# Two transfers for the fourth k-tile of each load, a moved sum in the seven-product blocks, and a buffer of its own for the next layer's norm

## The chip, the cores and the metric

The kernel runs on one core of a Trainium2 chip. The metric is the device time of one execution in microseconds, the median of several runs. The core has five engines with their own instruction streams: PE (matrix multiply), DVE (vector), ACT (scalar), POOL (GpSimd) and SP, which here only issues DMA transfers. An engine runs its stream in order, and waits on semaphores that other engines and transfers raise.

## The reference

```
x = x + attention(layernorm(x)); x = x + ffn(layernorm(x))      # this pair twice, same weights
attention: q = x @ wq (16 heads of 28), k = x @ wk, v = x @ wv (one key/value head of 28)
           softmax(q k^T / sqrt(28)) v for each head, then @ wo
ffn:       (silu(x @ w_gate) * (x @ w_up)) @ w_down
x: 2048 x 448, wq: 448 x 448, wk, wv: 448 x 28, w_gate, w_up: 448 x 1792, w_down: 1792 x 448, all float32
```

## The kernel before

**Numbers.** A float32 factor is carried as a rounded high part and a low part (the rest), and a product is high x high + high x low + low x high: `xh`, `xl` for activations, `wh`, `wl` (or `wgh`, `wgl`) for weights. `split` makes both parts on POOL.

**k-tiles.** The contraction length is 448 = 3 x 128 + 64. The fourth k-tile has only 64 rows, and is put into the 128 partitions twice: the upper copy turns into the low part (`flipped`, k = 3), so that one matmul of 128 rows does high and low together. `rows3` loads such a matrix: one transfer for the first three k-tiles, and a second one for the fourth, which reads the same 64 rows twice. It loads the gate and up weights (`columns`), the attention weights (`load_wqkv`) and, from DRAM, the transposed activations (`load` in `norm_steps`).

**Stages.** The tokens are four column groups c of 512. A layer has a projection stage (`Attention.project`, `product_T`: eleven matmuls for one of 16 (c, m) pairs), an attention stage of 256 steps, and a feed-forward stage in `groups` of two 128-column pieces of w_gate and w_up. In the attention stage ACT works nearly without a pause on the exponentials.

**Feed-forward.** The first two groups and the last one run as `unit` (group, c, piece): products into two banks, Silu into the one buffer `sg` on ACT (L1106), times up on DVE (L1107), high part `h` on ACT (L1108), low part on DVE (L1111), then the product with w_down (L345). `between` is a fence: ACT copies one column of a bank into `seen` (L352), and PE's next matmuls on the other rows of that bank wait for it. The four groups between are `mixed`: two column groups a, b at once in a seven-product (Strassen-Winograd) scheme, 16 blocks in a layer. The order within a block is the hand-written list `ORDER`; a name with one "-" at its end belongs to the block before, with two to the one before that, and each name goes to its engine in that order. A1 to A4 and S0 to S5 are products on the banks x, y, z, w (in pairs of 64 rows: the upper and lower half of the array), E and F the products with w_down. The sums out of the banks (C12, C22, C21; L859) run on DVE; C21 reads bank w, into which A2 of the next block writes. silB, mulB, hhB, hlB are the Silu, the product with up, the high part (ACT, L874) and the low part (DVE, L878) of column group b; silA, mulA, hhA, hlA those of a.

**Hand-over.** In the last group of layer 0 `hand_over(c)` prepares the next layer's first norm. For c = 0 it works on the side: statistics, `apply` (DVE, L254) and `turn` (a transpose on DVE, L259) through the buffer `sg`, `send` to DRAM (`xt`, L268), `load` back into `xn` by `rows3` (L128, L129), and `cut`, four casts on ACT into `xh` (L303), one k-tile each, with the low parts on DVE (L308, L311). `self.soon` says after how many units each step is issued. Behind `cut` in ACT's stream stand the `seen` copies of the next unit.

**Start.** Rows of x and the attention weights are loaded by SP in order, then the rows of c = 1 (`fill(1)`, L1250). PE runs idle transposes, transposes the norm of c = 0 (L295), then `project` for c = 0. `part` makes wh on ACT (L209) and wl on DVE (L210); z = 1 is the half that the first two projections use.

Of the kernel before, what the change touches and what calls it, by code (L numbers as in the profile page):

```python
# [8 lines left out]
F32 = mybir.dt.float32  # L9
F32R = mybir.dt.float32r  # L10
AF = mybir.ActivationFunctionType
ALU = mybir.AluOpType
# [3 lines left out]
P = 128  # L16
S = 2048
D = 448
# [34 lines left out]
def forward(  # L53
# [14 lines left out]
    nc = tc.nc  # L68
# [9 lines left out]
    pers = ctx.enter_context(tc.tile_pool(name="pers", bufs=1))  # L78
# [6 lines left out]
    phase, banks, threes, live, turn = ExitStack(), [], [], set(), {}  # L85
# [38 lines left out]
        nc.sync.dma_start(dst.bitcast(F32), src.bitcast(F32))  # L124

    def rows3(dst, src):
        n = src.shape[1]
        nc.sync.dma_start(dst[:, 0:3], src[0:384, :].rearrange("(k p) n -> p k n", p=P))  # L128
        nc.sync.dma_start(dst[:, 3], src[384:448, :][None].to_broadcast([2, 64, n]))  # L129

    def in_turn(cols):

# [18 lines left out]
    qraw = pers.tile([P, 512], F32, name="qraw")  # L151
# [33 lines left out]
    def load_wqkv(pool, first):  # L185


        wh = pool.tile([P, 4, 512], F32R, name="wh")
        wl = pool.tile([P, 4, 512], F32R, name="wl")

        def load(z):
            if first and not z:
                r = halves("wq2").bitcast(F32).rearrange("p a (b n) -> p (a b) n", n=256)
            else:
                r = wpool.tile([P, 4, 2, P], F32, name="wr").rearrange("p k b n -> p k (b n)")
            nc.gpsimd.memset(r[:, :, 252:256], 0.0)
            rows3(r[:, :, 0:224], wq[:, 224 * z : 224 * z + 224])
            rows3(r[:, :, 224:252], wk if z else wv)
            return r

        def part(z, r, k0=0, k1=4, only=None):
            ks = slice(k0, k1)
            hi, lo = (w[:, :, 256 * z : 256 * z + 256].rearrange("p k (b n) -> p k b n", b=2) for w in (wh, wl))
            for i, (cols, n0, n1) in enumerate(((r[:, ks, 0:224], 0, 112), (r[:, ks, 224:256], 112, 128))):
                if only not in (None, i):
                    continue
                raw = cols.rearrange("p k (b n) -> p k b n", b=2)
                if first:
                    nc.scalar.copy(hi[:, :, :, n0:n1], raw)  # L209
                    nc.vector.tensor_tensor(lo[:, :, :, n0:n1], raw, hi[:, :, :, n0:n1], ALU.subtract)  # L210
                else:
                    split(hi[:, ks, :, n0:n1], lo[:, ks, :, n0:n1], raw)

        if first:
            r1, r0 = load(1), load(0)
            return [lambda: part(1, r1), lambda: part(0, r0)], (wh, wl)
        raw = {}
        fs = []
        for z in (1, 0):
            fs.append(lambda z=z: raw.update({z: load(z)}))  # L220
            for kn in ((0, 2, 0), (2, 4, 0), (0, 4, 1)):
                fs.append(lambda z=z, kn=kn: part(z, raw[z], *kn))
        return fs, (wh, wl)
# [6 lines left out]
            again,  # L230
        )

    def norm_steps(c, away=False):


        got = {}
        cs = slice(4 * c, 4 * c + 4)

        def stat(t):
            nc.vector.bn_stats(stats[:, 4 * c + t, :], xres[:, 4 * c + t, :])  # L240
            nc.vector.bn_aggr(mv[:, 4 * c + t, :], stats[:, 4 * c + t, :])

        def scale():
            rstd = pers.tile([P, 4], F32, name="rstd", bufs=2)
            nc.gpsimd.tensor_scalar(rstd, mv[:, cs, 1], 1.0, EPS, ALU.mult, ALU.add)
            nc.gpsimd.tensor_tensor(rstd, rstd, halfn, ALU.pow)
            got["r"] = rstd

        def apply(t):
            if t == 0:  # L250
                got["x"] = pers.tile([P, 4, 512], F32, name="xn")
            got["o"] = (pers.tile([P, 512], F32, name="sg") if away else got["x"][:, t, :])[:, 0:D]
            i, r = xres[:, 4 * c + t, :], got["r"][:, t : t + 1]
            nc.vector.tensor_scalar(got["o"], i, mv[:, 4 * c + t, 0:1], r, ALU.subtract, ALU.mult)  # L254
            if not away:
                nc.gpsimd.tensor_copy(got["x"][:, t, D:512], got["o"][:, 384:D])

        def turn(t):
            nc.vector.transpose(side()[:, :, :, t], got["o"].rearrange("p (k s) -> p k s", s=32))  # L259

        def side():
            return got["x"].rearrange("p t n -> p (t n)")[:, 0 : 4 * D].rearrange("p (k s t) -> p k s t", s=32, t=4)

        def send():
            turns.append(dram.tile([D, 512], F32, name=f"xt{len(turns)}"))
            got["xt"] = turns[-1]
            for a in range(4):
                nc.sync.dma_start(  # L268
                    got["xt"].rearrange("(k r) n -> r k n", r=32)[:, :, P * a : P * a + P],
                    side()[32 * a : 32 * a + 32].rearrange("p k s t -> p k (s t)"),  # L270
                )

        def load():
            got["raw"] = pers.tile([P, 4, 512], F32, name="xn")
            rows3(got["raw"], got["xt"])

        got["load"] = load
        fs = [lambda t=t: stat(t) for t in range(4)] + [scale]
        for t in range(4):
            fs += [lambda t=t: apply(t)] + [lambda t=t: turn(t)] * away  # L280
        return fs + [send] * away, got

    turns = []

# [29 lines left out]

        return [(a[0][rs], b[0][rs]), (a[0][rs], b[1][rs]), (a[1][rs], b[0][rs])]

    def product_T(po, a_h, a_l, tiles):

        xh, xl = tiles[:2]
        seq = []  # L320
        for k in range(3):
            seq += [(a_h[k], xh[:, k, :]), (a_h[k], xl[:, k, :]), (a_l[k], xh[:, k, :])]
        seq += [(a_h[3], xh[:, 3, :]), (a_l[3], xh[:, 3, :])]
        for i, (a, b) in enumerate(seq):
            nc.tensor.matmul(po, a, b, start=(i == 0), stop=(i == len(seq) - 1))  # L325
# [30 lines left out]
    class Attention:  # L356
# [174 lines left out]
        def q(self, c, m):  # L531
            cs = slice(512 * c, 512 * c + 512)
            held, po = bank((3, 4, 5) if self.seen > len(self.order) - 4 else wide[-1], True)
            ms = slice(P * m, P * m + P)
            wh, wl = self.w
            product_T(po, [wh[:, k, ms] for k in range(4)], [wl[:, k, ms] for k in range(4)], self.X[c])
            if not full and self.seen in (6, 10, 14):
                self.maxima(self.seen // 4 - 1)
            live.remove(held)
# [3 lines left out]
            raw = pers.tile([P, 512], F32, name="sg") if last else self.pool.tile([P, 512], F32, name="stage")  # L543
# [45 lines left out]
        def scores(self, ff):  # L589
            next(switch)  # L590
            with tc.tile_pool(name=f"at{self.layer}", bufs=1, reuse_waits="tile") as wp:
# [123 lines left out]
                later = {}  # L715
                for c in range(3):
                    ff.X[c] = xtile(xpool) if c < 2 else None
                    fs, got = norm_steps(c, True)
                    n = NT * (4 * c + 5)
                    for kt, f in enumerate(fs):  # L720
                        later[n + kt] = f
                    later[n + 22] = got["load"]
                    for k in range(4) if c < 2 else ():
                        for z in range(2):
                            later[n + 34 + 2 * k + z] = lambda c=c, got=got, k=k, z=z: flipped(
                                ff.X[c], k, got["raw"][:, k, :], nc.vector.tensor_copy, (z,)
                            )
# [45 lines left out]
    HALVES = slice(0, 64), slice(64, 128)  # L773

    ORDER = (
        "A1 C21- Fc2-- Fp2-- mulA- A2 fY fX Fa0-- Fa1-- A3 fZ fW Fc3-- Fp3-- A4 s1 hhA- u2 E1- w1 w5 fE- u3 S0 "
        "hlA- gY E2- Ea0- Ea1- Ec2- Ep2- Ec3- Ep3- w2 S1 gX S2 gZ S3 gW S4 F1- C12 C22 silB mulB fF- S5 hhB hlB F2- silA"
    ).split()

    class FeedForward:  # L780
# [251 lines left out]
        def hand_over(self, c):  # L1032

            a = self.nxt
            fs, got = norm_steps(c, c == 0)
            for f in fs[:5]:
                f()
            a.pool = self.stage
            a.X[c] = xtile(xpool if c < 2 else self.xbp)

            def ready():
                for f in fs[5:]:
                    f()
                a.norms[c] = got

            if c == 0:
                self.soon.append([1, lambda: [f() for f in fs[5:9]]])
                self.soon.append([2, lambda: [f() for f in (*fs[9:], got["load"])]])
                self.soon.append([4, lambda: cut(got, a.X[c])])
                self.soon.append([5, lambda: [a.project() for _ in range(3)]])  # L1050
            elif c == 1:
                self.soon.append([2, ready])
            else:
                a.plan[4 * c - 4, 0] = [ready]
# [122 lines left out]
        def rest(self, xb):  # L1177
# [21 lines left out]
            for gi, fs in enumerate(groups):  # L1199
# [4 lines left out]
                if gi in mixed:  # L1204
                    self.blocked(gi)
                    if gi == mixed[-1]:
                        nc.gpsimd.memset(qraw, 0.0)
                        mixing.close()
                for c in range(NC) if gi not in mixed else ():
                    for n in range(len(fs)):  # L1210
# [28 lines left out]
    fs, got = norm_steps(0)  # L1239
# [28 lines left out]
    for c in range(1, NC):  # L1268
        fs, got = norm_steps(c)
        n = 4 * c - 4  # L1270
# [38 lines left out]
```

## Time and profile before

| | |
|---|---|
| median of 3 runs | 1973.86 us (1972.9 to 1975.1) |
| the profiled execution | 1975.62 us, of it 1973.8 us span from the first to the last instruction |
| granted TensorE clock, mean | 0.998 |
| PE busy | 1954.8 us, 99% of the span |
| ACT, DVE, POOL busy | 1339.0, 1028.5, 764.7 us |
| transfers | 79.67 MB; SP's queue takes 14.0% of the 16 DMA engines' span |

A row of the timeline gives the start and the duration in microseconds, engine, line, operation, output <- input, shapes, the count of merged instructions, and in brackets the idle time before it with what ended it. PEld is PE's weight load ahead of a matmul. A row of the waits gives total, times and the longest. A row of the stages by window gives the stretch and its length, busy time of PE, PEld, DVE, ACT and POOL (with instruction counts), the granted PE clock, the busy share of the 16 DMA engines and GB/s.

### The profile page before, as it was taken

What the parts mean: (1) busy time and instruction counts of PE and PEld (TensorE: products, weight loads), DVE (VectorE), ACT (ScalarE), POOL (GpSimd) and SP (SyncE); (2) the same over time, 40 slices, a digit from 0 to 9 for tenths busy, and PEclk for the clock granted to TensorE, in tenths of its full rate; (3) what the DMA queues carried; (4) which work ended last, traced back from release to release, by engine and by line L of the source; (5) the groups of instructions that cost most, each with busy time, mean ns of one, the idle gap of its engine ahead of it and who ended that gap; (6) DMA issues with size and microseconds to landing.
All of it is one profiled execution on the core that took longest, in us unless ns stands there. A gap on an engine that the chain in (4) does not pass through costs nothing. (4 is left out here: it accounts for less than half of the span.)

```text
span 1973.8 us, 45469 instructions
## 1 busy us (share of the span) xinstructions
PE 1954.8 (99%) x18315; PEld 1317.0 (67%) x18315; DVE 1028.5 (52%) x1713; ACT 1339.0 (68%) x2353; POOL 764.7 (39%) x988
## 2 busy tenths in 40 slices
PE   9999999999999999999899999999999999999998
PEld 7544545445458999999884445454454688999997
DVE  7444543544435566666554445435454346667653
ACT  4899897997954344444348998979979533444442
POOL 4212111132215768766332222111322157677640
PEclk9999999999999999999999999999999999999999
DMA  5101120121210110011131111101112101110102
GB/s 165 54 20 32 25 50 22 31 59 28 72 33 2 53 32 26 23 32 27 51 97 45 31 31 31 44 12 46 44 37 63 33 5 49 32 32 18 31 17 77
DMA packets 97630, 79.67 MB, mean 40 GB/s; under 512 B 23654, under 2 KB 80614, under 8 KB 97414
## 3 DMA queue, kind: packets, MB, share of 16 engines
q1 hardware_dynamic: 97126, 76.26, 14.0%
q8 instruction: 144, 2.36, 0.5%
q14 instruction: 72, 0.59, 0.1%
q10 hardware_dynamic: 288, 0.46, 0.1%
HBM read 57.15 MB, written 18.74 MB: 38 GB/s over the span
## 5 line engine op out<-in xcount | busy, mean ns | idle before, releaser
L669 PE MATMUL bank<-pt,vsb 128*32 128x512 f32 x4096 | 493.3, 598 | 0.3
L628 PE MATMUL bank<-qstack,keys 32*128 32x512 f32 x1536 | 484.7, 425 | 0.0
L628 PE MATMUL three<-qstack,keys 32*128 32x512 f32 x4608 | 460.3, 425 | 1.5 <-DVE vt L562 1.2
L628 PEld LDWEIGHTS three<-qstack,keys 32*128 32x128 f32 x4608 | 253.9, 182 | 295.4 <-ACT pt L641 179.4
L635 ACT ACTIVATE pt<-three 128x1536 f32<-128x1536 f32 x256 | 372.2, 1454 | 1.1 <-PE bank L669 0.8
L641 ACT ACTIVATE pt<-three 128x1536 f32<-128x1536 f32 x256 | 372.1, 1454 | 0.0
L345 PE MATMUL bank<-xh,wgh 64*128 64x512 f32 x1344 | 359.5, 393 | 6.3 <-ACT seen L352 5.8
L345 PE MATMUL bank<-wdh,h 64*128 64x448 f32 x1776 | 329.7, 364 | 0.4 <-ACT seen L352 0.3
L637 DVE COPY raw<-bank 128x512 f32<-128x512 f32 x256 | 177.5, 693 | 226.7 <-PE bank L628 224.9
L345 PE MATMUL bank<-xh,wgl 64*128 64x512 f32 x1020 | 288.9, 391 | 0.0
L679 DVE TENSOR_TENSOR o<-bank,o 128x512 f32<-128x512 f32 x224 | 155.0, 692 | 240.7 <-PE bank L669 235.8
L669 PEld LDWEIGHTS bank<-pt,vsb 128*32 128x32 f32 x4096 | 107.1, 109 | 249.6 <-issue 152.6
L708 POOL TENSOR_TENSOR o<-o 128x512 f32<-128x512 f32 x32 | 41.2, 1288 | 583.6 <-DMA o<-rd 474.4
L352 ACT COPY seen<-bank 128x1 f32<-128x1 f32 x788 | 99.3, 163 | 244.9 <-PE bank L345 184.4
L345 PE MATMUL bank<-xl,wgh 64*128 64x512 f32 x912 | 251.8, 391 | 0.0
L345 PEld LDWEIGHTS bank<-wdh,h 64*128 64x128 f32 x1776 | 238.1, 184 | 10.0 <-issue 2.0
L628 PEld LDWEIGHTS bank<-qstack,keys 32*128 32x128 f32 x1536 | 243.3, 183 | 1.2 <-DVE o L679 0.9
L345 PE MATMUL bank<-wdl,h 64*128 64x448 f32 x888 | 213.7, 367 | 0.0
L345 PEld LDWEIGHTS bank<-xh,wgh 64*128 64x128 f32 x1344 | 195.8, 185 | 19.0 <-ACT seen L352 6.2
L894 POOL TENSOR_TENSOR xres<-stage,xres 128x448 f32<-128x448 f32 x120 | 146.1, 1229 | 121.0 <-ACT stage L887 120.9
L640 ACT ACTIVATE pt<-bank 128x512 f32<-128x512 f32 x256 | 151.5, 592 | 59.8 <-PE bank L628 59.7
L859 DVE TENSOR_TENSOR xn<-bank,xn 128x512 f32<-128x512 f32 x192 | 126.4, 686 | 93.4 <-PE bank L345 76.0
(200 smaller groups left out, 3090.0 us busy)
## 6 DMA issues: line engine op xcount, KB each, us to landing
o<-rd SPq DMA_DIRECT2D x32, 256.0 KB
qraw<-qd SPq DMA_DIRECT2D x128, 56.0 KB
qd<-stage SPq DMA_DIRECT2D x30, 224.0 KB
xt<-xn SPq DMA_DIRECT2D x28, 224.0 KB
wdr<-in_B_w_down_dram SPq DMA_DIRECT2D x28, 224.0 KB
wr<-in_B_w_gate_dram SPq DMA_DIRECT2D x32, 192.0 KB
wr<-in_B_w_up_dram SPq DMA_DIRECT2D x32, 192.0 KB
xn<-xt SPq DMA_DIRECT2D x7, 768.0 KB
```

The lines of the kernel that those rows point to most:

```text
L345: nc.tensor.matmul(po, a, b, start=start, stop=stop, skip_group_check=True)
L352: nc.scalar.copy(seen[:, i : i + 1], po[:, 0:1])
L628: nc.tensor.matmul(three[:, j, :] if j < 3 else one, k[js, kp, ks], q[js, part, :], start=(z == 0), stop=(z == 2), tile_position=(32 * j, 0),)
L635: nc.scalar.activation(pt, three, AF.Exp, scale=SCALE)
L637: nc.vector.tensor_copy(raw, one)
L640: nc.scalar.activation(pt1, one, AF.Exp, scale=SCALE)
L641: nc.scalar.activation(pt, three, AF.Exp, scale=SCALE)
L669: nc.tensor.matmul(po[32 * j : 32 * j + 32, :], vsb[:, n % NT, :], pts[n][j], start=(n == 2 * d), stop=(n > 2 * d), skip_group_check=True,)
L679: nc.vector.tensor_tensor(acc, in_turn(po), acc, ALU.add)
L708: nc.gpsimd.tensor_tensor(rb, oraw, rb, ALU.mult)
L859: plus = lambda out, po, r: tt(by_tile(out), in_turn(po), by_tile(r), ALU.add)
L894: nc.gpsimd.tensor_tensor(r, h[e, t], r, ALU.add)
```

## The change

Four edits. (1) `rows3` loads the fourth k-tile by two transfers of 64 rows into the two partition halves, in place of one transfer that reads the 64 rows twice. (2) In `ORDER` hlB moves from its own block behind C21 of that block, which stands in the next block's list. (3) The first norm of the next layer goes through `qraw` in place of `sg`; the memset that `qraw` needs afterwards moves behind the `load` on POOL. (4) At the start wl of z = 1 is made on POOL in place of DVE, and the first projection of layer 0 takes its three matmuls with wl after the six with wh.

```diff
     def rows3(dst, src):
-        n = src.shape[1]
         nc.sync.dma_start(dst[:, 0:3], src[0:384, :].rearrange("(k p) n -> p k n", p=P))
-        nc.sync.dma_start(dst[:, 3], src[384:448, :][None].to_broadcast([2, 64, n]))
+        for rs in (slice(0, 64), slice(64, 128)):
+            nc.sync.dma_start(dst[rs, 3], src[384:448, :])
...
                     nc.scalar.copy(hi[:, :, :, n0:n1], raw)
-                    nc.vector.tensor_tensor(lo[:, :, :, n0:n1], raw, hi[:, :, :, n0:n1], ALU.subtract)
+                    eng = nc.gpsimd if z else nc.vector
+                    eng.tensor_tensor(lo[:, :, :, n0:n1], raw, hi[:, :, :, n0:n1], ALU.subtract)
...
-            got["o"] = (pers.tile([P, 512], F32, name="sg") if away else got["x"][:, t, :])[:, 0:D]
+            got["o"] = (away() if away else got["x"][:, t, :])[:, 0:D]
...
-    def product_T(po, a_h, a_l, tiles):
+    def product_T(po, a_h, a_l, tiles, late=False):
         xh, xl = tiles[:2]
-        seq = []
+        seq, low = [], []
         for k in range(3):
-            seq += [(a_h[k], xh[:, k, :]), (a_h[k], xl[:, k, :]), (a_l[k], xh[:, k, :])]
+            seq += [(a_h[k], xh[:, k, :]), (a_h[k], xl[:, k, :])]
+            (low if late else seq).append((a_l[k], xh[:, k, :]))
+        seq += low
         seq += [(a_h[3], xh[:, 3, :]), (a_l[3], xh[:, 3, :])]
...
-            product_T(po, [wh[:, k, ms] for k in range(4)], [wl[:, k, ms] for k in range(4)], self.X[c])
+            product_T(po, [wh[:, k, ms] for k in range(4)], [wl[:, k, ms] for k in range(4)], self.X[c], self.layer + self.seen == 0)
...
-        "A1 C21- Fc2-- Fp2-- mulA- A2 fY fX ...
+        "A1 C21- hlB- Fc2-- Fp2-- mulA- A2 fY fX ...
-        ... silB mulB fF- S5 hhB hlB F2- silA"
+        ... silB mulB fF- S5 hhB F2- silA"
...
-            fs, got = norm_steps(c, c == 0)
+            fs, got = norm_steps(c, None if c else lambda: qraw)
...
+            wipe = lambda: nc.gpsimd.memset(qraw, 0.0)
             if c == 0:
                 self.soon.append([1, lambda: [f() for f in fs[5:9]]])
-                self.soon.append([2, lambda: [f() for f in (*fs[9:], got["load"])]])
+                self.soon.append([2, lambda: [f() for f in (*fs[9:], got["load"], wipe)]])
...
                     if gi == mixed[-1]:
-                        nc.gpsimd.memset(qraw, 0.0)
                         mixing.close()
```

DVE's stream at the end of the first seven-product block of layer 0, before: C12 and C22 (L859, out of the second and third bank), mulB (L869), hlB (L878), C21 (L859, out of the fourth bank, w), two adds into the residual, mulA (L870).

```order
L859 TENSOR_TENSOR xn<-bank_7077,xn 128x512
L859 TENSOR_TENSOR xn<-bank_7078,xn 128x512
L869 TENSOR_TENSOR xn<-xn 128x512
L878 TENSOR_TENSOR h_8708<-xn,h_8708 128x512
L859 TENSOR_TENSOR xn<-bank_7079,xn 128x512
L1006 TENSOR_TENSOR xres<-bank_7080,xres 128x448
L1006 TENSOR_TENSOR xres<-bank_7081,xres 128x448
L870 TENSOR_TENSOR sg<-xn,sg 128x512
```

The same place now:

```order
L862 TENSOR_TENSOR xn<-bank_7091,xn 128x512
L862 TENSOR_TENSOR xn<-bank_7092,xn 128x512
L872 TENSOR_TENSOR xn<-xn 128x512
L862 TENSOR_TENSOR xn<-bank_7092,xn 128x512
L881 TENSOR_TENSOR h_8733<-xn,h_8733 128x512
L1009 TENSOR_TENSOR xres<-bank_7093,xres 128x448
L1009 TENSOR_TENSOR xres<-bank_7094,xres 128x448
L873 TENSOR_TENSOR sg<-xn,sg 128x512
```

C21 now stands directly behind mulB, and hlB behind C21; nothing else moved.

SP's stream at the start, before, behind the rows of x and the first three k-tiles of wq's half z = 1: the fourth k-tile, wk, then the half z = 0 with wv, then `fill(1)`.

```order
L129 DMA wr<-in_A_wq_dram 128x1x224
L128 DMA wr<-in_A_wk_dram 128x3x28
L129 DMA wr<-in_A_wk_dram 128x1x28
L128 DMA wq_144<-in_A_wq_dram 128x3x224
L129 DMA wq_144<-in_A_wq_dram 128x1x224
L128 DMA wq_144<-in_A_wv_dram 128x3x28
L129 DMA wq_144<-in_A_wv_dram 128x1x28
L1250 DMA xres<-in_A_x_dram 128x4x448
```

The same place now:

```order
L129 DMA wr<-in_A_wq_dram 64x224 x2
L127 DMA wr<-in_A_wk_dram 128x3x28
L129 DMA wr<-in_A_wk_dram 64x28 x2
L127 DMA wq_146<-in_A_wq_dram 128x3x224
L129 DMA wq_146<-in_A_wq_dram 64x224 x2
L127 DMA wq_146<-in_A_wv_dram 128x3x28
L129 DMA wq_146<-in_A_wv_dram 64x28 x2
L1253 DMA xres<-in_A_x_dram 128x4x448
```

Four transfers became eight ahead of `fill(1)`. The `rows3` call of the hand-over changes in the same way, one transfer of `xn<-xt` 128x1x512 into two of 64x512.

DVE's stream at the hand-over, before: the second pair of `apply` (L254) and `turn` (L259) of the next layer's norm, and then `sg` of the next unit.

```order
L254 TENSOR_SCALAR sg<-xres,mv,rstd 128x448
L259 STREAM_TRANSPOSE xn<-sg 128x448
L254 TENSOR_SCALAR sg<-xres,mv,rstd 128x448
L259 STREAM_TRANSPOSE xn<-sg 128x448
L1107 TENSOR_TENSOR sg<-bank_7078,sg 128x512
```

The same place now:

```order
L255 TENSOR_SCALAR qraw<-xres,mv,rstd 128x448
L260 STREAM_TRANSPOSE xn<-qraw 128x448
L255 TENSOR_SCALAR qraw<-xres,mv,rstd 128x448
L260 STREAM_TRANSPOSE xn<-qraw 128x448
L1111 TENSOR_TENSOR sg<-bank_7091,sg 128x512
```

The order is the same; only the buffer between `apply` and `turn` differs.

More of the change, by code (lines that the diff above doesn't have):

```diff
@@ L231, in xtile, with norm_steps @@
         )
-    def norm_steps(c, away=False):
+    def norm_steps(c, away=None):
         got = {}
@@ L279, in norm_steps @@
         for t in range(4):
-            fs += [lambda t=t: apply(t)] + [lambda t=t: turn(t)] * away
-        return fs + [send] * away, got
+            fs += [lambda t=t: apply(t)] + [lambda t=t: turn(t)] * bool(away)
+        return fs + [send] * bool(away), got
     turns = []
@@ L717, in scores @@
                     ff.X[c] = xtile(xpool) if c < 2 else None
-                    fs, got = norm_steps(c, True)
+                    fs, got = norm_steps(c, lambda: pers.tile([P, 512], F32, name="sg"))
                     n = NT * (4 * c + 5)
@@ L775, in forward @@
     ORDER = (
-        "A1 C21- Fc2-- Fp2-- mulA- A2 fY fX Fa0-- Fa1-- A3 fZ fW Fc3-- Fp3-- A4 s1 hhA- u2 E1- w1 w5 fE- u3 S0 "
-        "hlA- gY E2- Ea0- Ea1- Ec2- Ep2- Ec3- Ep3- w2 S1 gX S2 gZ S3 gW S4 F1- C12 C22 silB mulB fF- S5 hhB hlB F2- silA"
+        "A1 C21- hlB- Fc2-- Fp2-- mulA- A2 fY fX Fa0-- Fa1-- A3 fZ fW Fc3-- Fp3-- A4 s1 hhA- u2 E1- w1 w5 fE- u3 S0 "
+        "hlA- gY E2- Ea0- Ea1- Ec2- Ep2- Ec3- Ep3- w2 S1 gX S2 gZ S3 gW S4 F1- C12 C22 silB mulB fF- S5 hhB F2- silA"
     ).split()
```

## The prediction

> **What bounds the kernel now.** I read the page first.
>
> ```profile
> PE 1954.8 (99%) x18315; PEld 1317.0 (67%) x18315; DVE 1028.5 (52%) x1713; ACT 1339.0 (68%) x2353; POOL 764.7 (39%) x988
> ```
>
> PE works for all but 19.0 of 1973.8 us, and the change removes no matmul. So the change can only win what PE waits or what it works slowly, and can lose wherever a new wait reaches PE. Who makes PE wait is in the waits of PE over the whole run:
>
> ```profile
> PE bank L345 <- ACT seen L352: 6.1, 2, 5.8
> PE bank L1249 <- POOL ident masks.py:199: 1.9, 1, 1.9
> PE bank L345 <- DVE xn L859: 1.6, 5, 0.6
> ```
>
> The reader sees one wait of 5.8 us that outweighs all others. Narrowing the window finds it at the hand-over. Its timeline for PE, for ACT and for SP:
>
> ```profile
> 979.87 0.36 PE L345 MATMUL bank<-wdh,h 64*128 64x448 f32 x2
> 986.08 0.79 PE L345 MATMUL bank<-xh,wgh 64*128 64x512 f32 x2 [5.84 <-ACT seen L352]
> ...
> 980.03 1.66 ACT L303 CAST xh<-xn 128x512 fp32r<-128x512 f32 x3 [1.91 <-DMA xn<-xt]
> 985.29 0.62 ACT L303 CAST xh<-xn 128x512 fp32r<-128x512 f32 x1 [3.60 <-DMA xn<-xt]
> 985.81 0.54 ACT L352 COPY seen<-bank 128x1 f32<-128x1 f32 x6
> ...
> 969.04 3.05 SPq L268 DMA_DIRECT2D xt<-xn  x4
> 975.45 0.38 SPq L128 DMA_DIRECT2D xn<-xt  x1
> 975.88 0.51 SPq L129 DMA_DIRECT2D xn<-xt  x1
> ```
>
> PE waits for the fence copies `seen`; these stand on ACT behind the four casts of `cut`; the first three casts start when the first transfer has landed (980.03), the fourth waits another 3.60 us for the second transfer, a third of the first in size. The stages by window say why:
>
> ```profile
> 978.00:979.00 1.00, 1.00 (x12) 0.83 (x10) 1.00 (x2) 0.13 (x1) 1.00 (x2) 1.00 1.04 408
> 979.00:980.00 1.00, 1.00 (x13) 0.78 (x10) 0.93 (x5) 0.00 (x0) 1.00 (x2) 1.00 0.42 160
> 981.00:985.00 4.00, 0.00 (x0) 0.00 (x0) 2.21 (x5) 0.69 (x2) 1.90 (x2) 1.00 0.12 46
> 986.00:992.00 6.00, 5.92 (x28) 4.76 (x30) 3.02 (x6) 0.94 (x6) 1.45 (x4) 0.50 0.01 3
> ```
>
> While the fourth k-tile comes in, 0.12 of the 16 engines are busy, two of them, at 46 GB/s; one slice earlier all 16 moved 408 GB/s. The transfer that reads the 64 rows twice runs on two engines. The last row is the second half of the price: after the wait PE's granted clock is 0.50 for some 6 us.
>
> **The change part by part.** *(1) at the hand-over.* Two transfers of 64 rows (64 x 512 x 4 bytes, 128 KB each) come in place of one of 256 KB. Spread like the first transfer, they need 256 KB / 408 GB/s = 0.6 us of the engines. The engines get free at about 979.4 (0.42 of slice 979), so the rows are there by about 980.7, and the fourth cast starts behind the third, at 980.03 + 1.66 = 981.69, and not at 985.29. That takes 3.60 us off ACT and so off PE. What is late next is `xt`: the load is issued at 975.45 as before and the first three k-tiles land at 980.03. PE still waits, to 986.08 - 3.60 = 982.48. I take it that so short a wait leaves the clock alone: in this trace it was lost in a wait of 5.84 us. That gives back the half of 6 us, 3.0. Together 6.6 us. Bounds: 0 if the transfers are no quicker, 3.6 if the clock falls all the same.
>
> The Trainium skill speaks against this edit: "DMA: Bandwidth & Descriptors", section "Rules for kernel authors", says of two transfers to disjoint partition halves not to bother, since they serialize over the same 16 engines, and to use one of 128 partitions. By that sentence this term would be 0. The same section says that an outermost zero-stride broadcast of c copies confines a transfer to at most c engines, and the trace agrees with this second rule, with the 0.12 above; two halves in flight are in no trace here.
>
> *(3) own buffer.* ACT's Silu waited for the last `turn` to read `sg`, and DVE's product waited for that Silu. The row of DVE, and the next one of POOL:
>
> ```profile
> 969.74 0.69 DVE L1107 TENSOR_TENSOR sg<-bank,sg 128x512 f32<-128x512 f32 x1 [0.73 <-ACT sg L1106]
> 977.77 1.25 POOL L1010 TENSOR_TENSOR xres<-stage,xres 128x448 f32<-128x448 f32 x1 [10.17 <-ACT stage L1009]
> ```
>
> With `qraw` that 0.73 goes, but DVE's chain up to `turn` has no such wait in it, so `xt` and the load come no sooner: PE arrives up to 0.7 us earlier at the fence, and waits for it until 982.48, up to 2.9 us in all. I count 0. The memset behind the load stands on POOL inside the 10.17 us in which nothing is due.
>
> *(2) C21 ahead of hlB*, 32 blocks. The first one, DVE and PE, and the waits of the weight loads over the run:
>
> ```profile
> 707.55 0.36 PE L345 MATMUL bank<-wdh,h 64*128 64x448 f32 x1
> ...
> 707.58 0.69 DVE L869 TENSOR_TENSOR xn<-xn 128x512 f32<-128x512 f32 x1
> 709.08 0.69 DVE L878 TENSOR_TENSOR h<-xn,h 128x512 fp32r<-128x512 f32 x1 [0.81 <-ACT h L874]
> 709.69 0.68 DVE L859 TENSOR_TENSOR xn<-bank,xn 128x512 f32<-128x512 f32 x1
> ...
> 709.48 0.39 PE L345 MATMUL bank<-keys,kdiag 64*128 64x512 f32 x1
> 710.43 0.50 PE L345 MATMUL bank<-keys,kdiag 64*128 64x512 f32 x2 [0.56 <-DVE xn L859]
> ...
> PEld bank L345 <- DVE xn L859: 6.4, 18, 1.0
> ```
>
> A2 (710.43) may not write bank w before C21 (709.69) has read it; C21 stands behind hlB (709.08), and that waits for the cast hhB. But w was complete when S5 ended, at 707.55, and DVE was idle from 708.27. Moved ahead, C21 runs from about 708.3 to 709.0, in the gap, and A2 goes at its pace. hlB then starts at 709.08 as before. Its reader is E1, behind A2, A3 and A4, so a C21 that ends late still costs nothing there. Worth: at least PE's own waits, 1.6 us, at most those of its weight loads, 6.4. I take the middle, 4.0; here PE lost 0.95 less the usual 0.23 from pair to pair, 0.7 of that place's 1.0.
>
> *(4) and (1) at the start.* Rows of POOL, ACT, SP, DVE and PE, one stage, and a later piece of the same subtraction on POOL:
>
> ```profile
> 9.31 1.51 POOL L256 COPY xn<-xn 128x64 f32<-128x64 f32 x4 [0.61 <-DVE xn L254]
> 9.63 0.94 ACT L209 CAST wh<-wr 128x896 fp32r<-128x896 f32 x1 [7.25 <-DMA wr<-in_A_wq_dram]
> 10.54 2.19 SPq L1250 DMA_DIRECT2D xres<-in_A_x_dram  x1
> 10.61 1.36 DVE L210 TENSOR_TENSOR wl<-wr,wh 128x896 fp32r<-128x896 f32 x2
> 11.89 1.87 DVE L308 TENSOR_TENSOR xl<-bank,xh 128x512 fp32r<-128x512 f32 x3
> 14.55 0.49 PE L325 MATMUL bank<-xh,wh 128*128 128x512 f32 x1
> 17.27 0.63 DVE L240 BATCH_NORM_STATS2 stats<-xres 128x6 f32<-128x448 f32 x1 [0.55 <-DMA xres<-in_A_x_dram]
> 11.00:13.00 2.00, 1.83 (x15) 1.47 (x13) 2.00 (x4) 2.00 (x5) 1.74 (x7) 1.00 0.17 47
> 933.53 1.15 POOL L140 TENSOR_TENSOR wl<-wr,wh 128x448 fp32r<-128x448 f32 x1
> ```
>
> DVE is freed of 1.36 us ahead of xl, of which only some 0.3 counts, since xl also waits for the cast xh. POOL makes wl behind its copies, from 10.8, in about 2 x 1.15 + 0.4 = 2.7 us, so by 13.5; with the wl matmuls last, PE asks for it at about 13.6. Four more transfers stand on SP ahead of `fill(1)`, 4 x 0.51 = 2.0 us (the issue at 975.88), if the rest stays; but slice 11 to 13 shows again only two engines busy, and that goes. I count a gain of 0.3, between -2.0 and 1.4.
>
> *(1) elsewhere.* 79 transfers more (64 for w_gate and w_up: 28 pieces and 4 of them again, two matrices each; 8 for wq, wk and wv; 7 for `xn`), some 40 us of SP's time, on a queue that mostly waits. The loads of w_gate and w_up feed this group on POOL:
>
> ```profile
> L139 POOL TENSOR_SCALAR wgh<-wr 128x256 fp32r<-128x256 f32 x112 | 51.4, 459 | 0.0
> ```
>
> Its idle time is 0.0: no split ever waited for its load, so 0.5 us more of issue lies under that lead, and I count 0.
>
> Sum: 6.6 + 4.0 + 0.3 = 10.9. Against the profiled execution's 1975.62 that is 1964.7; this execution lay 1.76 above the median of the runs, so 1963.0.
>
> **The rivals.** *The clock still falls.* PE waits up to 2.9 us, and only one long wait is in this trace. Then 3.0 of the gain is lost: 1966.0. The Trainium skill, "TensorE: Matmul & The Clock Gate", section "Part 1: The HAM clock gate", gives an idle window of about 3.4 us as the condition; the wait of 5.84 agrees, and 2.9 would stay below it.
>
> *The halves serialize and win nothing*, the page's sentence as a mechanism here: the second half waits until the first has landed, and the fourth cast stays near 985.29. Then only 4.3 is left: 1969.6. For it: this trace shows no two halves in flight. Against it: the 408 GB/s that all 16 engines moved a slice earlier.
>
> *Both halves on one engine*, the slower side. If each 64-row transfer went to a single engine, the same for both, it would run at 46 / 2 = 23 GB/s: 256 KB take 11.4 us from 979.4, so the fourth cast starts at about 990.8, 5.5 late. The start would lose its 2.0 as well, the blocks give 4.0: 1973.86 + 5.5 + 2.0 - 4.0 = 1977.4, and 1979.8 with the blocks at 1.6. It decides from a landing behind 985.3. Against it: the four `xt` transfers of 32 partitions landed within 6.4 us, 969.04 to 975.45, for four times 224 KB (32 x 14 x 128 x 4 bytes).
>
> **How the numbers follow.** The forecast has 0.76, the fallen clock 0.10, no gain from the halves 0.07, one engine 0.04, and 0.03 are left for what I do not see. The forecast's own range: gains from 6.6 + 1.6 - 2.0 = 6.2 to 6.6 + 6.4 + 1.4 = 14.4, so 1959.5 to 1967.7. It holds the fallen clock too; to reach 8 in 10 it goes on to the halves without gain, 1969.6. A measurement here can tell about 0.2%, 3.9 us, from no change. The forecast and the fallen clock lie below 1969.9, the third case on that edge, and I count half of it: faster 0.89, same 0.07, slower 0.04.
>
> **What would show it.** Right: the fourth cast directly behind the third; PE's wait for `seen` at 2 to 3 us and no slice with clock 0.50 behind it; the waits for L859 in the blocks (line moved by three) nearly gone; the first statistics of c = 1 no later than 17.3. Wrong: two or fewer engines busy behind the first `xn` transfer, a new wait of PE in the blocks for hlB or E1, or PE waiting for wl from POOL in the first projection.

## The result, and the profile after

The changed kernel takes 1966.89 us (median of 6 runs, 1965.81 to 1967.42), the kernel before, in runs on the same chip, 1973.51 us (6 runs): a ratio of 0.9964, 95% interval 0.9952 to 0.9977. That is faster by some 6.6 us. The forecast was 1963.0 with a range of 1959.5 to 1969.6: the side and the range hold, the time lies 3.9 us above the forecast, and the gain is 6.6 us where 10.9 was put. The profiled execution took 1967.23 us, 8.4 less than the one of before.

The page's engines, then the waits of PE over the run; here and in after's other rows the lines have moved by one to four (L345 is L348, L352 is L355, L859 is L862, L878 is L881):

```profile
PE 1950.6 (99%) x18315; PEld 1322.2 (67%) x18315; DVE 1012.1 (51%) x1711; ACT 1338.4 (68%) x2353; POOL 769.3 (39%) x989
```

```profile
PE bank L348 <- ACT seen L355: 3.5, 1, 3.5
PE bank L1252 <- POOL ident masks.py:199: 1.9, 1, 1.9
PE three L631 <- DVE vt L565: 1.2, 2, 0.6
```

The 1.6 us of PE for the sum `xn` are gone, and so are the 6.4 us of its weight loads: neither list has a row for L862. The wait at the hand-over has shrunk from 5.84 to 3.47 us. Its timeline for SP, ACT and PE:

```profile
972.84 0.38 SPq L127 DMA_DIRECT2D xn<-xt  x1
973.27 1.13 SPq L129 DMA_DIRECT2D xn<-xt  x2
...
977.94 2.18 ACT L304 CAST xh<-xn 128x512 fp32r<-128x512 f32 x4 [3.24 <-DMA xn<-xt]
...
980.03 0.53 ACT L355 COPY seen<-bank 128x1 f32<-128x1 f32 x6
...
980.29 0.79 PE L348 MATMUL bank<-xh,wgh 64*128 64x512 f32 x2 [3.47 <-ACT seen L355]
...
986.63 0.50 PE L328 MATMUL bank<-xh,wh 128*128 128x512 f32 x1
```

The four casts now stand in one row: the fourth needs no landing of its own. But they start 5.10 us after the issue of the first transfer (972.84 to 977.94), where it was 4.58 (975.45 to 980.03). The windows show what the engines did meanwhile:

```profile
975.00:976.00 1.00, 1.00 (x12) 0.98 (x10) 0.97 (x4) 0.00 (x0) 1.00 (x2) 1.00 1.01 393
976.00:977.00 1.00, 0.81 (x8) 0.43 (x5) 0.97 (x3) 0.00 (x0) 0.70 (x1) 1.00 1.06 410
977.00:978.00 1.00, 0.00 (x0) 0.00 (x0) 0.93 (x4) 0.06 (x1) 0.00 (x0) 1.00 0.84 148
```

The halves keep all 16 engines busy at about 400 GB/s, at the same time as the first transfer, which lands half a microsecond later. That the one causes the other is what the runs with and without the halves show, at the end of this document. And the clock fell again. These two windows, which lie on the edges of its fall, have the granted clock in the third column from the end, behind POOL:

```profile
975.76:979.17 3.41, 1.05 (x11) 0.67 (x8) 2.74 (x8) 1.23 (x3) 1.91 (x3) 1.00 0.63 192
979.17:982.58 3.41, 2.29 (x10) 1.81 (x12) 3.34 (x8) 1.39 (x8) 0.95 (x3) 0.50 0.02 5
```

### The profile page after: what moved, and what is told of

Same layout as the page of the kernel before. It is cut to its first block, busy times and chain, and to the rows that moved or that the text cites. A ratio compares the mean times of both kernels' runs of the same rounds, so it can differ in the third digit from the quotient of the medians.

```text
span 1965.5 us, 45651 instructions
## 1 busy us (share of the span) xinstructions
PE 1950.6 (99%) x18315; PEld 1322.2 (67%) x18315; DVE 1012.1 (51%) x1711; ACT 1338.4 (68%) x2353; POOL 769.3 (39%) x989
## 5 line engine op out<-in xcount | busy, mean ns | idle before, releaser
L348 PE MATMUL bank<-xh,wgh 64*128 64x512 f32 x1344 | 360.5, 393 | 3.8 <-ACT seen L355 3.5
L348 PE MATMUL bank<-wdh,h 64*128 64x448 f32 x1776 | 327.0, 364 | 0.1
L348 PE MATMUL bank<-xh,wgl 64*128 64x512 f32 x1020 | 289.7, 391 | 0.0
L355 ACT COPY seen<-bank 128x1 f32<-128x1 f32 x788 | 99.1, 163 | 240.9 <-PE bank L348 180.8
L348 PE MATMUL bank<-xl,wgh 64*128 64x512 f32 x912 | 251.9, 391 | 0.0
L348 PEld LDWEIGHTS bank<-wdh,h 64*128 64x128 f32 x1776 | 231.6, 184 | 8.9 <-issue 2.0
L348 PE MATMUL bank<-wdl,h 64*128 64x448 f32 x888 | 208.2, 366 | 0.0
L348 PEld LDWEIGHTS bank<-xh,wgh 64*128 64x128 f32 x1344 | 196.1, 185 | 16.1 <-ACT seen L355 3.9
L897 POOL TENSOR_TENSOR xres<-stage,xres 128x448 f32<-128x448 f32 x120 | 151.5, 1274 | 113.2 <-ACT stage L890 113.2
L862 DVE TENSOR_TENSOR xn<-bank,xn 128x512 f32<-128x512 f32 x192 | 126.5, 687 | 127.2 <-PE bank L348 94.3
```

What stands on the lines that cost most here:

```text
L348: nc.tensor.matmul(po, a, b, start=start, stop=stop, skip_group_check=True)
L355: nc.scalar.copy(seen[:, i : i + 1], po[:, 0:1])
L862: plus = lambda out, po, r: tt(by_tile(out), in_turn(po), by_tile(r), ALU.add)
L897: nc.gpsimd.tensor_tensor(r, h[e, t], r, ALU.add)
```

## The experiments

All ratios are to the kernel before on the same chip; a difference "by the ratio" is worked out from them, since the kernel before itself has medians of 1973.51 to 1975.04 us beside them. Theory T was formed on the two traces: the gain is the shorter wait at the hand-over and the order in the blocks, and nothing else. The table has, for each profiled run, the time between the starts of the same matmuls of PE: the hand-over stretch (960.02 to 1025.51 in the kernel after), the blocks of layer 0 (700.07 to 940.12) and of layer 1 (1690.03 to 1930.16); then PE's longest wait for `seen` there, and how long the granted clock stood at 0.50 behind it, all in us.

| kernel | ratio, 95% interval | hand-over | blocks 0 | blocks 1 | wait | clock at 0.50 |
|---|---|---|---|---|---|---|
| before | 1 | 68.85 | 243.00 | 241.05 | 5.84 | 6.83 |
| after | 0.9964, 0.9952 to 0.9977 | 65.48 | 240.05 | 240.13 | 3.47 | 6.83 |
| edit 1 alone | 0.9973, 0.9963 to 0.9983 | 62.87 | 242.37 | 241.34 | 2.69 | none |
| edit 2 alone | 0.9979, 0.9970 to 0.9988 | 69.04 | 240.50 | 240.30 | 5.96 | 6.83 |
| edit 3 alone | 0.9997, 0.9988 to 1.0006 | 67.99 | 242.66 | 240.96 | 6.78 | 6.83 |
| edit 4 alone | 0.9997, 0.9988 to 1.0006 | 68.36 | 242.12 | 241.05 | 5.91 | 6.83 |
| after, first load in three | 0.9952, 0.9938 to 0.9965 | 63.26 | 239.99 | 240.19 | 2.41 | 3.41 |
| after without edit 3 | 0.9963, 0.9949 to 0.9976 | 63.16 | 240.01 | 240.22 | 2.84 | none |
| after, old load at the hand-over | 0.9981, 0.9972 to 0.9990 | 68.09 | 240.15 | 240.20 | 6.70 | 6.83 |
| after, casts on DVE | 0.9935, 0.9922 to 0.9949 | 59.42 | 240.11 | 240.15 | none | none |
| before, casts on DVE | 0.9957, 0.9943 to 0.9970 | 60.88 | 242.38 | 240.93 | 0.27 | none |
| edits 2 to 4, casts on DVE | 0.9932, 0.9919 to 0.9946 | 60.90 | 240.17 | 240.33 | none | none |
| edits 1 and 2, casts on DVE | 0.9932, 0.9919 to 0.9946 | 60.16 | 239.99 | 240.53 | 0.27 | none |

### Each edit alone

The loads (edit 1):

```diff
-        nc.sync.dma_start(dst[:, 3], src[384:448, :][None].to_broadcast([2, 64, n]))
+        for rs in (slice(0, 64), slice(64, 128)):
+            nc.sync.dma_start(dst[rs, 3], src[384:448, :])
```

> The kernel before with edit 1 alone (the fourth k-tile by two transfers of 64 rows). Theory T (the change wins at the hand-over, 3.4 us in the trace of the kernel after, and in the blocks, 5.0 us; PE waits there because ACT's seen stands behind the fourth cast): about 3.5 us faster than before, with the fourth cast directly behind the third; 6.5 us if the clock stays up, since without edit 3 PE comes later and waits some 2.8 us. Rival L (the other 78 loads win too, by less sharing of the transfer engines): 5 us or more, with PE earlier than before already ahead of the hand-over. Rival R (the 64-row halves win nothing and the gain is all in the order of the blocks): no change.

1968.84 us against 1974.6, 5.3 us by the ratio. That lies between the two values of theory T; the profiled run won 6.0 us in its hand-over stretch (68.85 to 62.87) and kept its clock. Two of its nine timed runs, the slowest (1970.64 and 1970.71), have a mean granted clock of 0.998 and not 0.999 or more, so there the clock fell too. Rival R falls. Rival L's condition, PE earlier ahead of the hand-over, isn't to be had from one stage: layer 0's blocks took 242.37, inside what the kernels without edit 2 took (242.12 to 243.00). It is tested below.

The order (edit 2):

```diff
-        "A1 C21- Fc2-- ...  S5 hhB hlB F2- silA"
+        "A1 C21- hlB- Fc2-- ...  S5 hhB F2- silA"
```

> The kernel before with edit 2 alone (hlB behind C21). Theory T: 5.0 us faster (3.1 in layer 0, 1.9 in layer 1, as the two traces show by the start of the same matmul), the waits of PE and of its weight loads for the sum C21 nearly gone, the hand-over as before with its wait of 5.8 us and its slower clock. The prediction's term would give 4.0 us, with bounds of 1.6 and 6.4. Rival L: 2 us or less, the rest of those 5.0 belonging to the loads of w_gate and w_up that lie in the same stretches.

1970.46 us, 4.1 us by the ratio (2.4 to 5.9), with the hand-over as before. The table gives the size more closely: layer 0's blocks take 242.12 to 243.00 in the five kernels without this edit and 239.99 to 240.50 in the eight with it, layer 1's 240.93 to 241.34 and 240.13 to 240.53. The means differ by 2.4 and 0.8: 3.2 us. The 5.0 of the first two traces held some scatter. Rival L falls: the two kernels with edit 2 and the old loads have 240.50 and 240.17 in layer 0, near the 239.99 to 240.15 of those with the halves. (In DVE's stream now, as listed ahead of the prediction, the first two sums read `bank_7090` and `bank_7091`; `bank_7092` is w, which C21 alone reads.) One block of the kernel after, DVE and PE:

```profile
707.96 0.69 DVE L872 TENSOR_TENSOR xn<-xn 128x512 f32<-128x512 f32 x1
...
708.57 0.68 DVE L862 TENSOR_TENSOR xn<-bank,xn 128x512 f32<-128x512 f32 x1
...
709.34 0.69 DVE L881 TENSOR_TENSOR h<-xn,h 128x512 fp32r<-128x512 f32 x1
...
709.86 0.65 PE L348 MATMUL bank<-keys,kdiag 64*128 64x512 f32 x4
```

C21 (L862) fills the gap that DVE had, hlB (L881) begins right behind it, and the matmul row of A2 has no bracket any more.

The buffer (edit 3) and the start (edit 4):

```diff
-            fs, got = norm_steps(c, c == 0)
+            fs, got = norm_steps(c, None if c else lambda: qraw)
...
```

> The kernel before with edit 3 alone (the next layer's first norm through qraw). Theory T: no change in time; PE comes up to 0.7 us earlier to the fence at the hand-over and waits that much longer, some 6.5 us in place of 5.84. Rival B (the buffer wins by itself, since the whole chain of the hand-over is ahead): 0.7 us faster or more, with the load issued earlier than 975.4.

1973.81 us against 1974.6: no change that can be measured (by the ratio 0.6 us, from 2.4 faster to 1.2 slower). The load was issued at 974.58 and not at 975.45, but this run was as much earlier already at the start of the stretch (961.81 for 962.68), so the chain is no shorter; PE came to the fence sooner and waited 6.78 us in place of 5.84, and passed it 23.47 us behind the start of the stretch, before 23.40. The interval leaves room for rival B's 0.7 us, but the shorter chain that was to bring it is not there.

```diff
-                    nc.vector.tensor_tensor(lo[:, :, :, n0:n1], raw, hi[:, :, :, n0:n1], ALU.subtract)
+                    eng = nc.gpsimd if z else nc.vector
+                    eng.tensor_tensor(lo[:, :, :, n0:n1], raw, hi[:, :, :, n0:n1], ALU.subtract)
...
-        product_T(po, ..., self.X[c])
+        product_T(po, ..., self.X[c], self.layer + self.seen == 0)
```

> The kernel before with edit 4 alone (wl of the first projections on POOL, its matmuls last). Theory T: the start wins 0 to 0.3 us, no change that can be measured. Rival S (the edit wins at the start, but edit 1 took it back by the five more issues on SP ahead of the rows of x): 1 us faster or more. Rival P (POOL's subtraction comes too late for the first projection): 0.5 us or more slower, with a wait of PE for wl.

1973.63 us: no change that can be measured, with the same interval, and no wait of PE for wl, so rival P falls. Rival S's 1 us lies inside the interval, but the trace does not have it: PE starts the attention stage at 60.03, before at 60.17, and between 59.76 and 60.51 in all 13 profiles.

### What is left of the wait, and the clock

The first transfer of the hand-over's load in three pieces (the condition picks this one load):

```diff
-            rows3(got["raw"], got["xt"])
+            if c or len(turns) != 4:
+                return rows3(got["raw"], got["xt"])
+            for k in range(3):
+                nc.sync.dma_start(got["raw"][:, k], got["xt"][P * k : P * k + P, :])
+            for rs in (slice(0, 64), slice(64, 128)):
+                nc.sync.dma_start(got["raw"][rs, 3], got["xt"][384:448, :])
```

> The kernel after, with the first three k-tiles of the hand-over's load as three transfers of 128 x 512 in place of one. Theory T (PE waits because the casts on ACT start only when the first transfer of 0.75 MB has landed, 5.1 us after its issue): the first cast starts some 1 us earlier, the wait at the fence falls from 3.47 to about 2.5 us: 1.0 us faster, and 4 us if the clock then stays up. Rival I (two more issues on SP, each some 0.5 us, push the fourth k-tile back): the last cast starts later than in the kernel after, 0.5 to 1 us slower.

1964.47 us, 0.9952: some 2.4 us below the kernel after by the ratios, with intervals that overlap. Rival I falls; the wait fell by the forecast 1.0 us. But the clock fell all the same, behind a wait of 2.41 us; ACT, PE and two windows:

```profile
975.00 1.27 ACT L309 CAST xh<-xn 128x512 fp32r<-128x512 f32 x2 [0.86 <-DMA xn<-xt]
977.35 1.14 ACT L309 CAST xh<-xn 128x512 fp32r<-128x512 f32 x2 [1.08 <-DMA xn<-xt]
...
978.67 0.79 PE L353 MATMUL bank<-xh,wgh 64*128 64x512 f32 x2 [2.41 <-ACT seen L360]
```

```profile
975.05:978.46 3.41, 1.21 (x12) 0.82 (x9) 3.27 (x10) 2.30 (x6) 1.93 (x3) 1.00 0.45 148
978.46:981.87 3.41, 3.20 (x16) 2.52 (x18) 3.27 (x7) 0.47 (x7) 2.30 (x5) 0.50 0.02 5
```

The change without edit 3 (the norm goes through `sg`, as before):

```diff
-            fs, got = norm_steps(c, None if c else lambda: qraw)
+            fs, got = norm_steps(c, c == 0)
...
```

> The kernel after without edit 3 (the next layer's first norm through sg again). Theory T: PE comes 0.7 us later to the fence and goes on at the same time, so no change if the clock falls here too. Rival C (edit 3 made the wait longer, 3.47 in place of about 2.8 us, and that cost the clock; without it the prediction's term of 3.0 us for the clock comes true): 3 us faster, with no slice of clock 0.50 behind the hand-over.

Here a longer wait, 2.84 us, left the clock alone, in this kernel and with 2.69 us in the one with edit 1 alone. Two windows of this kernel, then of that one:

```profile
976.18:979.59 3.41, 1.58 (x16) 1.08 (x12) 3.27 (x10) 1.34 (x3) 2.01 (x3) 1.00 0.56 154
979.59:983.00 3.41, 2.40 (x20) 1.99 (x22) 3.34 (x8) 1.28 (x8) 2.21 (x5) 1.00 0.02 5
```

```profile
976.89:980.30 3.41, 2.17 (x22) 1.56 (x18) 3.27 (x10) 0.96 (x3) 2.08 (x2) 1.00 0.71 218
980.30:983.71 3.41, 1.96 (x18) 1.61 (x19) 3.34 (x7) 1.72 (x9) 2.13 (x3) 1.00 0.03 7
```

So it is not the length of the wait alone that decides. All clock changes of a run lie on a grid of 3.41 us: the stretches between two changes last 3.413, 6.827, 972.798, 976.212 and 979.625 us, which is 1, 2, 285, 286 and 287 times 3.413. The grid lies otherwise in each run. In every profile here the clock fell, at the hand-over or when PE's work ended, at the end of a grid window in which PE was busy for 1.37 us (40%) or less, and at the end of none with 1.56 us (46%) or more. The window with 1.37 us stands at the end of the run with edit 2 alone; its last column but two is the clock in it, and in the window behind it:

```profile
1962.46:1965.87 3.41, 1.37 (x7) 0.92 (x5) 2.04 (x4) 0.00 (x0) 0.00 (x0) 1.00 0.54 196
1965.87:1969.29 3.42, 0.00 (x0) 0.00 (x0) 0.00 (x0) 0.00 (x0) 0.00 (x0) 0.50 0.24 85
```

The waits of 2.84 and 2.69 us were cut by an edge of the grid; the 2.41 us lay, but for 0.2, within one window. From the fence to the end of the hand-over stretch PE takes 42.6 us here, as with edit 1 alone, and 45.2 in the kernel after, 2.6 us more. In the six profiles with a fall of 6.83 us it is 44.5 to 45.5, so by the traces such a fall costs 1.9 to 2.8 us.

Each timed run also has its mean granted clock. It is 0.997 or 0.998 in the profiled runs with a fall of 6.83 us at the hand-over, and 0.999 or 1.000 in those with a shorter fall or none. By this mark the clock fell in four of the six runs of the kernel after (1967.1 us on average), in one of five here (1968.1) and in two of nine with edit 1 alone (1970.7). In the others it fell for 3.41 us at most; they took 1966.0, 1966.3 and 1968.6 us on average, 1.1 to 2.1 us less.

The median of the change without edit 3, 1966.74 us, is hardly below after's. With intervals of 2.6 us on each side, rival C's 3 us are improbable. Whether edit 3 makes a fall more frequent, four of six with it and one of five without, stays open with so few runs.

The change with the old load at this one place:

```diff
-            rows3(got["raw"], got["xt"])
+            if c or len(turns) != 4:
+                return rows3(got["raw"], got["xt"])
+            nc.sync.dma_start(got["raw"][:, 0:3], got["xt"][0:384, :].rearrange("(k p) n -> p k n", p=P))
+            nc.sync.dma_start(got["raw"][:, 3], got["xt"][384:448, :][None].to_broadcast([2, 64, 512]))
```

> The kernel after, with the hand-over's load alone as in the kernel before (the fourth k-tile by one transfer that reads the 64 rows twice); the other 78 loads keep the two halves. Theory T: 3.4 us slower than the kernel after, the wait of the fourth cast of some 3.6 us back and PE's wait at the fence some 6.5 us. Rival L (the gain of edit 1 is in the other loads): within 1 us of the kernel after.

1970.45 us, 3.4 us above the kernel after by the ratios. ACT and PE at the hand-over:

```profile
977.03 1.66 ACT L307 CAST xh<-xn 128x512 fp32r<-128x512 f32 x3 [2.69 <-DMA xn<-xt]
982.37 0.62 ACT L307 CAST xh<-xn 128x512 fp32r<-128x512 f32 x1 [3.67 <-DMA xn<-xt]
...
983.16 0.80 PE L351 MATMUL bank<-xh,wgh 64*128 64x512 f32 x2 [6.70 <-ACT seen L358]
```

What edit 1 wins, it wins at this one load of 79: with the old load there the kernel has the ratio of edit 2 alone (0.9981 and 0.9979), and the other 78 are worth nothing that can be measured. Rival L falls.

### The casts off ACT's queue

If ACT's queue is what PE pays for, the casts need only go elsewhere:

```diff
-                self.soon.append([4, lambda: cut(got, a.X[c])])
+                self.soon.append([4, lambda: cut(got, a.X[c], copy=nc.vector.tensor_copy)])
```

> The kernel after, with the four casts of the hand-over on DVE in place of ACT (0.42 us each, as 16 of DVE's casts of that shape took), so that ACT's seen copies no longer stand behind the load. Theory T (the whole price of the hand-over is ACT's queue: PE's 3.47 us and 3.0 of the clock): the wait for seen is gone, the projection begins at about 980.2 in place of 986.6 with xl of the first k-tile ready at 979.0, 6 us faster than the kernel after, about 1961. Rival W (the wait moves to the projection, because DVE's casts and subtractions together take some 4.3 us, or to the next unit's product on DVE): 3 us faster or less, with a new wait of PE for xl or sg.

1961.31 us (1960.97 to 1962.06), 0.9935: 5.7 us below the kernel after by the ratios. ACT, DVE and PE:

```profile
976.39 0.29 ACT L355 COPY seen<-bank 128x1 f32<-128x1 f32 x3 [0.45 <-PE bank L348]
...
977.57 0.43 DVE L304 CAST xh<-xn 128x512 fp32r<-128x512 f32 x1
978.04 0.69 DVE L309 TENSOR_TENSOR xl<-xn,xh 128x512 fp32r<-128x512 f32 x1
...
979.80 0.49 PE L328 MATMUL bank<-xh,wh 128*128 128x512 f32 x1
...
981.23 0.69 DVE L312 TENSOR_TENSOR xh<-xn,xh 64x512 fp32r<-64x512 f32 x1
```

`seen` follows PE's banks at once, PE no longer waits for it, and the projection begins at 979.80 (986.63 in the kernel after). A cast costs 0.43 us on DVE and 0.62 on ACT. Rival W's new wait did not come. Then the same line on the kernel before, and with parts of the change:

> The kernel before with nothing changed but the four casts of the hand-over, on DVE in place of ACT; the fourth k-tile still comes on two engines. Theory Q (what PE pays at the hand-over is ACT's queue, not the landing itself): PE passes the fence at 980.2 and has 3.9 us of the unit's matmuls before the projection, whose fourth k-tile is asked for at about 986.2, when the late landing and DVE's cast and subtraction are just done (985.2 + 0.42 + 0.69): the wait of 5.84 and the slower clock go, 8 us faster than before. Rival D (the landing itself is the price): DVE stands behind the late k-tile as ACT did, PE waits for it in the projection, and the gain is 4 us or less.

1966.76 us against 1975.04, 0.9957: 8.5 us by the ratio, from this one line, as much as the four edits together bring, though the fourth k-tile comes as late as ever. DVE and PE:

```profile
984.69 0.43 DVE L303 CAST xh<-xn 128x512 fp32r<-128x512 f32 x1 [0.76 <-DMA xn<-xt]
...
985.90 0.50 PE L325 MATMUL bank<-xh,wh 128*128 128x512 f32 x1 [0.55 <-DVE xh L311]
```

Of PE's wait, 0.55 us is left. Theory Q holds, rival D falls.

> The kernel after with the casts of the hand-over on DVE, and without edit 1: all loads read the 64 rows twice, as before. Theory Q: PE comes to the projection at 979.8 and asks for the fourth k-tile at 981.9; load issued at 972.4, landing 9.7 us later, cast and subtraction done at 983.2: a wait of 1.3 us in the projection, about 1.3 us slower than the kernel with edit 1 and the casts on DVE (1961.3). Rival L (edit 1 is worth several us by its other loads): 3 us slower or more.

1962.2 us, 0.9932; PE waits for the fourth k-tile once:

```profile
983.11 0.50 PE L328 MATMUL bank<-xh,wh 128*128 128x512 f32 x1 [1.41 <-DVE xh L312]
```

The wait is the forecast one (1.41 for 1.3). The median lies 0.9 above 1961.31, and the ratios show no difference. Rival L falls again.

> Edits 1 and 2 with the casts of the hand-over on DVE, without edits 3 and 4. Theory T (edits 3 and 4 are worth nothing): within 0.7 us of the kernel with all four edits and the casts on DVE (1961.3). Rival M (with the fence out of the way, edit 3's earlier chain counts, since the projection now waits for DVE): 1 us slower or more.

1961.8 us, 0.9932: edits 3 and 4 bring nothing here that can be measured. In the trace the hand-over stretch is 0.7 us longer than with all four edits (60.16 for 59.42), so rival M's 1 us is not reached, but so few runs do not exclude it. The three kernels with edit 2 and the casts on DVE cannot be told apart; they are faster than both kernels of this case.

## Why the prediction was right, and where it was off

**The fourth cast directly behind the third:** right. The 3.60 us behind the third cast are gone, and the kernel with the old load at the hand-over has 3.67 again. PE passes the fence 20.27 us behind the start of the stretch in place of 23.40: 3.1 us, where 3.6 was put. The Trainium skill ("DMA: Bandwidth & Descriptors", section "Rules for kernel authors") advises against two transfers to disjoint halves, since they use the same 16 engines. That they do is what the slices of 393 and 410 GB/s show; but here the halves stand in for a transfer on two engines, so the advice, by which this term would be 0, did not carry over. Both rivals on the halves fall.

**What is late next:** nearly. The load was the next to come, as said, but the first three k-tiles landed 5.10 us after the issue and not 4.58, since the halves share the engines with them. The step took the first transfer's time over as it was, and that is the 0.5 us by which the fence came later than forecast.

**"So short a wait leaves the clock alone":** this step failed, in the profiled run. The wait was 3.47 us, above the 2.9 that were put as the most, by the 0.5 of the later landing, and the clock fell. The term of 6.6 measured 3.4, by the table's hand-over column; with the clock up, edit 1 alone measured 6.0. The fall costs 2.6 us in after's trace and 1.1 to 2.1 between timed runs, where 3.0 was put. The rival with the fallen clock, 1966.0 us, given a chance of 0.10, is the one that came, 0.9 below the median and in four of the six runs. The range was worked out from bounds on the blocks and the start, and holds the time by that width; the prediction says itself that it takes in the fallen clock too. The two runs with the clock at 0.999, 1965.81 and 1966.24 us, did not reach 1963.0 either. Where the reasoning went wrong is that it compared lengths of waits; what fits all the runs is how much of one 3.41 us window PE works, and no edit sets where the window lies. The Trainium skill ("TensorE: Matmul & The Clock Gate", section "Part 1: The HAM clock gate") has the free-running window of 3.4 us, and the falls of 3.41 and 6.83 us agree; an idle window as the condition does not: 31%, 35% and 40% of work in it did not save the clock.

**The blocks:** the mechanism was right at every step (C21 in DVE's gap, hlB no later, A2 without its wait); the term of 4.0 measured 3.2 over 13 profiles, inside its bounds of 1.6 and 6.4. S5's last product ends at 707.90 and not at 707.55, but DVE is not free before 708.27 either way.

**The start:** 0.3 was put, nothing was measured. The steps came as described (first statistics of c = 1 at 15.86, before 17.3), but PE's start of the attention stage, 60.18 us, is that of before, 60.17.

**Edit 3 and the loads elsewhere at 0:** right, as far as the intervals tell, but for edit 3's open share in the clock (edit 3 alone; edits 1 and 2 with the casts on DVE; the old load at the hand-over; edits 2 to 4 with the casts on DVE).

The rest of the difference between the two profiled runs, 8.4, is scatter: layer 1's attention stage (from the end of the hand-over stretch to the start of layer 1's blocks) took 666.23 us before and 664.52 after, and 664.31 to 666.03 in the other eleven, with no relation to any edit. No run here explains it.

## What to carry to other kernels

When PE waits for a tiny copy, look at what stands ahead of it in its engine's queue before making that faster: moving four casts to an engine with time to spare was worth as much as all four edits, within the intervals, and left of the faster transfer's gain nothing that can be measured. A transfer whose outermost step is a repeat of two kept two of the 16 engines busy; it matters only where somebody waits for its landing, at one place of 79 here. Do not count a shorter wait as a kept clock: count PE's work in the window of 3.41 us that is placed worst.

## What the runs showed of the hardware that was not expected

The clock was lost behind a wait of 2.41 us and kept behind one of 2.84. Over the 13 profiles it fell after windows of 3.41 us with PE busy for 1.37 us at most, and did not after windows with 1.56 us or more; where between them the limit lies, and whether it is the busy time that counts, is not settled, since no run set the grid's place. A transfer that follows on the same queue delays the landing of the first: 4.55 to 4.68 us from issue to the first cast with a follower on two engines (before, edits 2, 3 and 4 alone, old load at the hand-over), 5.10 to 5.31 with two followers on all 16 (after, edit 1 alone, after without edit 3).
